# Decode attention with a gated GeGLU: w_gate loaded ahead of wq, the first keys in two loads

## The chip, the cores and the metric

The kernel runs on one core of a Trainium2 chip. Its time is the device time of one execution in microseconds (us); a profiled execution shows where the time goes. Engines: TensorE (PE; PEld is its weight load), VectorE (DVE), ScalarE (ACT), GpSimd (POOL) and SyncE (SP), which here issues nearly all transfers.

## The reference

```
x [4, 1, 512]; k_cache, v_cache [4, 32, 4096, 128]; wq [512, 4096]; wo [4096, 512]
w_gate, w_up [512, 1792]; w_down [1792, 512]; gate_w [512]; all float32

q = (x @ wq) as [4, 32, 1, 128]
p = softmax(q . k_cache / sqrt(128))
a = (p . v_cache) as [4, 1, 4096] @ wo
b = (gelu_tanh(x @ w_gate) * (x @ w_up)) @ w_down
g = sigmoid(sum(x * gate_w))
out = g * a + (1 - g) * b
```

## The kernel before

The caches are 537 of the 565 MB that are read. They are cut into NT = 32 pieces of keys and 32 of values, 8.39 MB each: piece i holds four heads of one batch row, as 128 partitions x 16384 elements (128 rows of 128). The texts call the loads k0, k1, ... and v0, v1, ...

All big data live in one tile `big` with 45056 elements per partition. A key piece lies at 0 (even i) or 12288 (odd i); so two neighbours share the quarter from 12288 to 16384. The values lie at VA = 28672. A step's work on its keys is split for this: `products(i, True)` and `sums(i, True)` multiply the shared quarter by the query and add up (VectorE), then SP issues the load of k(i+1), which overwrites it, and `products(i, False)` and `sums(i, False)` do the other three quarters. `soft_max(i)` then makes the weights, on VectorE and ACT. `pv(i - 1)` multiplies the values by them on TensorE, and v(i) is issued when it is done, into the same place.

Before the first step: `q_project` (x @ wq, 64 matmuls on TensorE), four operations on VectorE (L347 to L352, and L368), `q_spread` (TensorE) and a copy to the tile `qb` (ACT, L374), after which the first product (L384) can start. The feed-forward's `ffn_up(0)` and `ffn_up(1)` (x @ w_gate, x @ w_up, 32 matmuls each, L518), `gates` and `ffn_gelu` (L530 to L537) stand inside step 0, between its two sums.

wq lies in the place of the values. w_gate and w_up go into the same place, so their loads wait for `q_project`. v0 goes there too and waits for `ffn_gelu`. The results of `ffn_up` go to `fu`, two pieces of `big` behind w_up.

A planner (`Plan`) writes the program: each engine's instructions stand in the order in which they are called, and every step gets the semaphore waits that its reads and writes of places in tiles need. SP issues its loads in the written order too, so a load that waits holds up those behind it. All loads are put on one queue, shared by 16 DMA engines.

Of the kernel before, what the change touches and what calls it, by code (L numbers as in the profile page):

```python
# [8 lines left out]
AF = mybir.ActivationFunctionType  # L9
OP = mybir.AluOpType  # L10
# [122 lines left out]
def tile_gated_mix(tc: tile.TileContext, x, kc, vc, wq, wo, w_gate, w_up, w_down, gate_w, out):  # L133
    nc = tc.nc
    P = 128
    B, H, S, D = kc.shape
    DM = x.shape[2]
    F = w_gate.shape[1]
    KC = DM // P
# [6 lines left out]
    TW = R * D  # L146
    RO = R // 4
    RJ = 4
    BP = 2
    FG = F // 4  # L150
    FC = F // P
    HW = 16
    E = HW * D // P
# [15 lines left out]
    def sb(pool, name, shape):  # L169
        sizes[name] = math.prod(shape[1:])  # L170
        return pool(name, [P] + list(shape[1:]), F32).ap()[:shape[0]]
# [6 lines left out]
    KB_, VA = TW - RO * D, 2 * TW - RO * D  # L178
# [8 lines left out]
    half = sb(consts, "half", [P, 1])  # L187
# [14 lines left out]
    O = [sb(consts, f"o{n}", [P, RJ, D]) for n in range(B // BP)]  # L202
# [6 lines left out]
    q = sb(ps, "q", [P, B, D])  # L209
# [3 lines left out]
    sm = sb(ps, "sm", [P, D + 1])  # L213
    sg = sb(ps, "sg", [P, KC * B])

    Q0, F0, F1, W0, D0 = VA, VA, VA + KC * F, VA, VA + TW // 2
    W1, ES = TW, TW + TW // 2
    GS = VA - 6 * DM
    XS, U0, QD, FU, FT, OXA = VA - 2 * DM, VA - 4 * DM, VA - DM, VA + 2 * KC * F, ES + 2 * E * 32, ES + 2 * E * 32 + DM

    def place(a, n):
        return big[:, a:a + n]

    def z(a, n):
        return ("big", a, a + n)

    def t(*names):
        return [(n, 0, sizes[n]) for n in names]
# [3 lines left out]
    x_sb, gw = place(XS, DM)[:B], place(GS, DM)[:B]  # L232
    u = place(U0, 2 * DM).rearrange("p (s n) -> p s n", s=2)
    qd = place(QD, D)
    fu = place(FU, 2 * DM).rearrange("p (s n) -> p s n", s=2)
    OX32 = place(OXA, E * GW * HT * D // E)[:32].rearrange("q (e g h k) -> q e g h k", e=E, g=GW, h=HT)
    OX = OX32[:B * HT]
    oV = place(FT, E * 32).rearrange("p (e m) -> p e m", e=E)
# [5 lines left out]
    V, A, T, G = nc.vector, nc.scalar, nc.tensor, nc.gpsimd  # L244

    def dve(emit, reads, writes):
        return add("dve", emit, reads, writes)

    def act(emit, reads, writes):
        return add("act", emit, reads, writes)  # L250

    def pe(emit, reads, writes):
        return add("pe", emit, reads, writes)
# [4 lines left out]
    def load(dst, src, writes, lane):  # L258
        return add("sp", lambda: nc.sync.dma_start(dst, src), (), writes, lane=lane, unit=16)

    def load_kv(kind, i):
        src = (vc, kc)[kind == "k"]
        a = KB_ * (i % 2) if kind == "k" else VA if i < NT - 1 else 0
        s = src[i % B, HT * (i // B):HT * (i // B) + HT].rearrange("h (p r) d -> (h p) (r d)", p=PH)
        load(place(a, TW), s, [z(a, TW)], "vl" if kind == "v" and i == NT - 1 else kind)

    def KA(i):
# [5 lines left out]
    def load_f(s):  # L273
        load(place((F0, F1)[s], KC * F), (w_gate, w_up)[s].rearrange("(p c) n -> p (c n)", c=KC),
             [z((F0, F1)[s], KC * F)], f"f{s}")
# [4 lines left out]
    def load_w(w):  # L280
# [4 lines left out]
        if w:  # L285
            for h in range(2):
                for e in range(WO_END[w][-1], E):
                    n0, m = e * DM + COLS[2 * h][0], COLS[2 * h + 1][1] - COLS[2 * h][0]
                    load(place(W1 + n0, m), src[:, n0:n0 + m], [z(W1 + n0, m)], f"e{h}{e % 2}")

    load(place(Q0, KC * H * D), wq.rearrange("(p c) n -> p (c n)", c=KC), [z(Q0, KC * H * D)], "q")
    add("act", lambda: nc.scalar.dma_start(x_sb, x.rearrange("b s d -> (b s) d")), (), [z(XS, DM)], lane="x0", unit=16)
    add("act", lambda: nc.scalar.dma_start(gw, gate_w.rearrange("(s n) -> s n", s=1).to_broadcast([B, DM])), (),
# [61 lines left out]
    def gates():  # L355
        pe(lambda: T.matmul(sm[:, :B], ones[:B], gd, start=True, stop=True), t("ones", "gd"), [("sm", 0, B)])
        act(lambda: A.activation(g4, sm[:, :B], AF.Exp, scale=-1.0), [("sm", 0, B)], t("g4"))
        dve(lambda: V.tensor_scalar(g4, g4, 1.0, None, op0=OP.add), t("g4"), t("g4"))
        dve(lambda: V.reciprocal(g4, g4), t("g4"), t("g4"))
        dve(lambda: V.tensor_tensor(g16.rearrange("p (j b) -> p j b", b=B), m16.rearrange("p (j b) -> p j b", b=B),  # L360
                                    g4[:, None, :].to_broadcast([P, 4, B]), op=OP.mult), t("m16", "g4"), t("g16"))
        dve(lambda: V.tensor_reduce(g1, g16, axis=AX.X, op=OP.add), t("g16"), t("g1"))
        dve(lambda: V.tensor_scalar(half, g1, -0.5, 0.5, op0=OP.mult, op1=OP.add), t("g1"), t("half"))
        dve(lambda: V.tensor_tensor(gmask, g4[:, :, None].to_broadcast([P, B, HT]),
                                    pmask[:, None, :].to_broadcast([P, B, HT]), op=OP.mult), t("g4", "pmask"), t("gmask"))

    def q_pick(g):
        dve(lambda: V.tensor_scalar(HC, hmask[:, bass.ds(row(g - 1) * HT + HT, HT), None].to_broadcast([P, HT, PH]), 1.0,  # L368
                                    None, op0=OP.mult), t("hmask"), t("hc"))

    def q_spread():
        pe(lambda: T.matmul(q.rearrange("p b d -> p (b d)"), HC.rearrange("p h k -> p (h k)"),  # L372
                            QM.rearrange("p b d -> p (b d)"), start=True, stop=True), t("hc", "QM"), t("q"))
        act(lambda: A.activation(QB, q, AF.Copy), t("q"), t("qb"))  # L374
# [4 lines left out]
    def products(i, shared):  # L379
        b = i % B  # L380
        r0, r1 = rows(i, shared)
        k = place(KA(i), TW).rearrange("p (r d) -> p r d", d=D)[:, r0:r1]
        m = [z(KA(i) + r0 * D, (r1 - r0) * D)]
        dve(lambda: V.tensor_tensor(k, k, QB[:, b:b + 1, :].to_broadcast([P, r1 - r0, D]), op=OP.mult),  # L384
            m + t("qb"), m)

    def sums(i, shared):
        r0, r1 = rows(i, shared)
        k = place(KA(i), TW).rearrange("p (r d) -> p r d", d=D)[:, r0:r1]
        dve(lambda: V.tensor_reduce(SC[i % 2][:, r0:r1], k, axis=AX.X, op=OP.add),  # L390
            [z(KA(i) + r0 * D, (r1 - r0) * D)], [(f"sc{i % 2}", r0, r1)])
# [30 lines left out]
    def gather_a(i):  # L422
        n = i // BP % 2
        act(lambda: A.activation(O[n], PO[n], AF.Copy), t(f"po{n}"), t(f"o{n}"))  # L424
# [89 lines left out]
    def ffn_up(s):  # L514
        def emit():
            for c in range(KC):
                for j in range(4):
                    last = T.matmul(q.rearrange("p b d -> p (b d)")[32 * j:32 * j + 32, :FG], xTf[:, c, :32],  # L518
                                    place((F0, F1)[s] + c * F + j * FG, FG), start=c == 0, stop=c == KC - 1)
            return last  # L520

        pe(emit, t("xT") + [z((F0, F1)[s], KC * F)], t("q"))
        act(lambda: A.activation(fu[:, s, :FG], q.rearrange("p b d -> p (b d)")[:, :FG], AF.Copy),
            t("q"), [z(FU + s * DM, FG)])

    def ffn_gelu():
        x1, r1 = fu[:, 0, :FG], [z(FU, FG)]
        (t1, z1), (t2, z2), (t3, z3), (th, z4), (y, z5), (v, z6) = (
            (place(F1 + a * DM, FG), [z(F1 + a * DM, FG)]) for a in range(6))
        dve(lambda: V.tensor_tensor(t1, x1, x1, op=OP.mult), r1, z1)  # L530
        dve(lambda: V.tensor_scalar(t2, t1, 0.044715, 1.0, op0=OP.mult, op1=OP.add), z1, z2)
        dve(lambda: V.tensor_tensor(t3, t2, x1, op=OP.mult), z2 + r1, z3)
        act(lambda: A.activation(th, t3, AF.Tanh, scale=c_gelu), z3, z4)
        dve(lambda: V.scalar_tensor_tensor(y, th, 1.0, x1, op0=OP.add, op1=OP.mult), z4 + r1, z5)  # L534
        dve(lambda: V.scalar_tensor_tensor(v, y, half, fu[:, 1, :FG], op0=OP.mult, op1=OP.mult),  # L535
            z5 + t("half") + [z(FU + DM, FG)], z6)
        dve(lambda: V.transpose(hT, v.rearrange("p (k i) -> p i k", i=FC)), z6, t("hT"))  # L537

    def ffn_down(f0, f1):
# [1 line left out]
            a = D0 + f * DM  # L541
            project_wide(hT[:, f, :], place(a, DM), [("hT", f * 32, f * 32 + 32), z(a, DM)])

    load_f(0)
    load_f(1)
    q_pick(0)
    q_spread()
    for i in range(NT):
        g, b = divmod(i, B)
        plan.turn = (i - 1) // B if 0 < i < NT - B + 1 else None  # L550
        if b == 1 and g + 1 < NG:
            q_pick(g + 1)
        products(i, True)
        sums(i, True)
        if i < NT - 1:
            load_kv("k", i + 1)
        else:
            load_kv("v", i)
        products(i, False)
        if i == 0:  # L560
            gates()
            ffn_up(0)
            ffn_up(1)
            ffn_gelu()
            load_kv("v", 0)
        sums(i, False)
        if i > 0:
            pv(i - 1)
            if i < NT - 1:
                load_kv("v", i)  # L570
            if i % BP == 0:
                gather_a(i - 1)
            if b == 0:
                gather(g - 1)
            if b == 3 and g + 1 < NG:
                q_spread()
        soft_max(i)
        if i > 0 and b == 0:
            weigh(g - 1)
# [25 lines left out]
    for h in range(2):  # L605
        for e in range(WO_END[1][-1], E):
            s, w, reads = attended(1, e)
# [52 lines left out]
```

## Time and profile before

| | |
|---|---|
| time, median of 3 runs | 1308.96 us (1308.88 to 1309.77) |
| the profiled execution | 1308.95 us, its span 1307.5 us |
| busy: VectorE | 1158.2 us |
| busy: TensorE, its weight loads | 353.2, 100.2 us |
| busy: ACT | 87.3 us |
| transfers | 564.83 MB, 432 GB/s over the span |

The span is the part of an execution that the trace covers, 1.45 us shorter than the time. Busy times of different engines overlap.

### The profile page before, as it was taken

The page shows a single profiled execution, that of the slowest core. Times are in us where ns is not written, and L with a number is a line of the kernel's source. Part 1 is how long each engine was busy: PE and PEld are TensorE (multiplying, and loading weights), DVE is VectorE, ACT ScalarE, POOL GpSimd, SP SyncE. Part 2 cuts the span into 40 slices and gives each one's busy share as a digit, 9 for nine tenths or more (in the row PEclk, how much of TensorE's full clock was granted, in tenths as well). Part 3 has the DMA queues.
Part 4 walks back from the last instruction along what each step waited for, and adds up shares of the span by engine and source line. Part 5 has one row for each costly group of instructions (what it writes and reads, how often), then busy time and mean ns, then how long its engine had stood idle before and what let it go on. Part 6 is the DMA issues. An engine that isn't in the chain of part 4 may idle for free.

```text
span 1307.5 us, 6158 instructions
## 1 busy us (share of the span) xinstructions
PE 353.2 (27%) x2512; PEld 100.2 (8%) x2512; DVE 1158.2 (89%) x303; ACT 87.3 (7%) x291; POOL 0.7 (0%) x6
## 2 busy tenths in 40 slices
PE   2303233212232211322321222321133232123227
PEld 0100001000010000100000000100001000000003
DVE  2799999999899998989989898998989899898992
ACT  0000000000000000000000000000000000000001
POOL 0000000000000000000000000000000000000000
PEclk9656666556666656666655666665666665666668
DMA  9999999999999999999999999999999999999998
GB/s 418 424 439 439 430 441 428 439 427 441 425 441 425 441 427 439 435 433 439 431 439 429 439 427 441 425 441 425 441 433 433 439 431 439 431 439 428 439 428 370
DMA packets 10986, 564.83 MB, mean 432 GB/s; under 512 B 1232, under 2 KB 1752, under 8 KB 1888
## 3 DMA queue, kind: packets, MB, share of 16 engines
q1 hardware_dynamic: 10960, 564.67, 99.8%
q8 instruction: 7, 0.11, 0.0%
q14 instruction: 3, 0.02, 0.0%
q10 hardware_dynamic: 16, 0.02, 0.0%
HBM read 564.67 MB, written 0.01 MB: 432 GB/s over the span
## 4 chain that ended last, share of the span: by engine, by line
DMA 72%; DVE 26%; PE 1%; issue 1%; ACT 0%; SPq 0%; DVEq 0%
DMA big<-in_A_k_cache 66%; DVE sc L390 13%; DVE big L384 12%; DMA big<-in_B_w_up 2%; DMA big<-in_A_wo 2%; DMA big<-in_A_wq 2%; PE po L330 1%; PE q L518 0%; PE acc L505 0%; PE wide L497 0%; PE po L505 0%; DVE hT L537 0%; DVE big L535 0%; DVE big L530 0%; DVE big L534 0%
## 5 line engine op out<-in xcount | busy, mean ns | idle before, releaser
L384 DVE TENSOR_TENSOR big<-big,qb 128x4096 f32<-128x4096 f32 x64 | 556.0, 8687 | 89.5 <-DMA big<-in_A_k_cache 89.5
L390 DVE TENSOR_REDUCE sc<-big 128x32 f32<-128x4096 f32 x64 | 555.9, 8686 | 2.3
L416 PE MATMUL po<-big,PM 128*32 128x512 f32 x2048 | 295.9, 743 | 899.9 <-DMA big<-in_A_v_cache 899.9
L416 PEld LDWEIGHTS po<-big,PM 128*32 128x32 f32 x2048 | 72.7, 133 | 1116.7 <-DMA big<-in_A_v_cache 823.9
L402 ACT ACTIVATE PM<-sc,nb 32x128 f32<-32x128 f32 x128 | 67.2, 525 | 476.4 <-DVE nb L397 430.7
L424 ACT ACTIVATE o<-po 128x512 f32<-128x512 f32 x16 | 9.6, 597 | 446.2 <-PE po L416 446.2
L402 ACT ACTIVATION_READ_ACCUMULATOR PM<-sc,nb 32x1 f32 x128 | 26.1, 204 | 0.0
L374 ACT ACTIVATE qb<-q 128x512 f32<-128x512 f32 x8 | 4.8, 597 | 245.7 <-PE q L372 245.7
L347 DVE TENSOR_TENSOR big<-po,amask 128x512 f32<-128x512 f32 x2 | 1.3, 686 | 18.0 <-PE po L330 18.0
L433 PE MATMUL sm<-o,sel 128*16 128x128 f32 x128 | 15.4, 273 | 5.8 <-ACT o L424 5.8
L518 PE MATMUL q<-big,xT 128*32 128x448 f32 x64 | 9.5, 751 | 18.0 <-DMA big<-in_B_w_gate 13.0
L330 PE MATMUL po<-big,xT 128*32 128x512 f32 x64 | 8.7, 702 | 18.9 <-DMA big<-in_A_wq 18.9
L433 PEld LDWEIGHTS sm<-o,sel 128*16 128x16 f32 x128 | 11.7, 97 | 14.4 <-ACT o L424 13.1
L615 DVE COPY res<-acc 4x144 f32<-4x144 f32 x1 | 0.3, 296 | 12.7 <-PE acc L505 12.7
L372 PE MATMUL q<-QM,hc 128*128 128x512 f32 x16 | 9.3, 666 | 4.2 <-DVE hc L368 4.2
L395 DVE TENSOR_REDUCE m<-sc 128x1 f32<-128x128 f32 x32 | 9.2, 286 | 1.1
L440 DVE RECIPROCAL ri<-sm 16x1 f32<-16x1 f32 x8 | 1.2, 156 | 8.7 <-PE sm L435 8.7
L396 DVE STREAM_TRANSPOSE mt<-m 128x32 f32<-128x32 f32 x32 | 6.8, 212 | 1.1
L397 DVE TENSOR_REDUCE nb<-mt 128x1 f32<-128x32 f32 x32 | 5.9, 186 | 1.1
L497 PE MATMUL wide<-big 128*32 128x512 f32 x46 | 5.6, 596 | 1.9 <-DMA big<-in_A_wo 1.9
L320 DVE TENSOR_TENSOR big<-big 4x512 f32<-4x512 f32 x1 | 0.7, 679 | 4.8 <-DMA big<-in_gate_w 4.8
L518 PEld LDWEIGHTS q<-big,xT 128*32 128x32 f32 x64 | 2.9, 146 | 23.8 <-issue 23.8
(74 smaller groups left out, 59.8 us busy)
## 6 DMA issues: line engine op xcount, KB each, us to landing
big<-in_A_wo SPq DMA_DIRECT2D x1, 4096.0 KB, 28.3
big<-in_B_w_gate SPq DMA_DIRECT2D x1, 3584.0 KB, 18.9
big<-in_B_w_up SPq DMA_DIRECT2D x1, 3584.0 KB, 28.1
big<-in_B_w_down SPq DMA_DIRECT2D x1, 3584.0 KB, 19.0
big<-in_A_wo SPq DMA_DIRECT2D x1, 1792.0 KB, 26.4
big<-in_A_wo SPq DMA_DIRECT2D x1, 1280.0 KB, 29.1
big<-in_A_k_cache SPq DMA_DIRECT2D x32, 29.7
big<-in_A_v_cache SPq DMA_DIRECT2D x32, 29.3
```

Of the source, the lines that this page charges most:

```text
L330: last = T.matmul(PO[s][32 * j:32 * j + 32].rearrange("p j d -> p (j d)"), xTf[:, c, :32], w[:, n0:n0 + HB * D], start=c == 0, stop=c == K ...
L372: pe(lambda: T.matmul(q.rearrange("p b d -> p (b d)"), HC.rearrange("p h k -> p (h k)"), QM.rearrange("p b d -> p (b d)"), start=True, sto ...
L384: dve(lambda: V.tensor_tensor(k, k, QB[:, b:b + 1, :].to_broadcast([P, r1 - r0, D]), op=OP.mult), m + t("qb"), m)
L390: dve(lambda: V.tensor_reduce(SC[i % 2][:, r0:r1], k, axis=AX.X, op=OP.add), [z(KA(i) + r0 * D, (r1 - r0) * D)], [(f"sc{i % 2}", r0, r1)])
L395: dve(lambda: V.tensor_reduce(M1[n], SC[n], axis=AX.X, op=OP.max), t(f"sc{n}"), t(f"m1{n}"))
L396: dve(lambda: V.transpose(MT, M1[n].to_broadcast([P, PH])), t(f"m1{n}"), t("mt"))
L397: dve(lambda: V.tensor_reduce(NB[n], MT, axis=AX.X, op=OP.max, negate=True), t("mt"), t(f"nb{n}"))
L402: last = A.activation(PM[:, PZ:].rearrange("p (c m) -> p c m", m=32)[s, :, h:RJ * HT:HT], SC[n][s, :].rearrange("p (c j) -> p c j", j=RJ), ...
L416: last = T.matmul(PO[n][32 * c:32 * c + 32].rearrange("p j d -> p (j d)"), PM[:, m0:m0 + 32], place(VAT(i) + j * N, N), start=b == 0 and j ...
L424: act(lambda: A.activation(O[n], PO[n], AF.Copy), t(f"po{n}"), t(f"o{n}"))
L433: T.matmul(sm[:B * HT, :D], selv[:, j, m0:m0 + B * HT], O[n][:, j, :], start=(n, j) == (0, 0), stop=(n, j) == (N - 1, RJ - 1))
L518: last = T.matmul(q.rearrange("p b d -> p (b d)")[32 * j:32 * j + 32, :FG], xTf[:, c, :32], place((F0, F1)[s] + c * F + j * FG, FG), start ...
```

## The change

w_gate (`load_f(0)`) is issued first of all, ahead of wq; it goes to the place F0 = TW = 16384, inside the place of k1, which is free until then. Behind wq, k0 comes in two loads: the shared quarter (elements 12288 to 16384 of each row), which the first product reads, and the other three quarters. w_up alone waits for `q_project` and goes to VA. `ffn_up(0)` is written right behind the first `q_spread`. The results of `ffn_up` go to the tiles `o0` and `o1`, which `gather_a` fills in later steps.

```diff
-    Q0, F0, F1, W0, D0 = VA, VA, VA + KC * F, VA, VA + TW // 2
+    Q0, F0, F1, W0, D0 = VA, TW, VA, VA, VA + TW // 2
...
-    fu = place(FU, 2 * DM).rearrange("p (s n) -> p s n", s=2)
+    fu = [O[s].rearrange("p j d -> p (j d)")[:, :FG] for s in range(2)]
...
+        if kind == "k" and i == 0:
+            for c0, c1 in ((TW - RO * D, TW), (0, TW - RO * D)):
+                load(place(a + c0, c1 - c0), s[:, c0:c1], [z(a + c0, c1 - c0)], "k" if c0 else "k0")
+            return
         load(place(a, TW), s, [z(a, TW)], "vl" if kind == "v" and i == NT - 1 else kind)
...
+    load_f(0)
     load(place(Q0, KC * H * D), wq.rearrange("(p c) n -> p (c n)", c=KC), [z(Q0, KC * H * D)], "q")
...
-        act(lambda: A.activation(fu[:, s, :FG], q.rearrange("p b d -> p (b d)")[:, :FG], AF.Copy),
-            t("q"), [z(FU + s * DM, FG)])
+        act(lambda: A.activation(fu[s], q.rearrange("p b d -> p (b d)")[:, :FG], AF.Copy),
+            t("q"), [(f"o{s}", 0, FG)])
...
-    load_f(0)
     load_f(1)
     q_pick(0)
     q_spread()
+    ffn_up(0)
...
         if i == 0:
             gates()
-            ffn_up(0)
             ffn_up(1)
             ffn_gelu()
             load_kv("v", 0)
```

The first loads on SP, before (in_A_k_cache is k0, then k1 and k2; in_A_v_cache is v0; lane_pe and lane_dve are the semaphores that TensorE and VectorE raise):

```order
L259 DMA big<-in_A_wq 128x16384
L259 DMA big<-in_A_k_cache 128x16384
L627 UNCONDITIONAL_BRANCH
L259 DMA big<-in_B_w_gate 128x7168 [waits barrier_Pool_Activation_PE_DVE_SP_release,lane_pe]
L259 DMA big<-in_B_w_up 128x7168
L259 DMA big<-in_A_k_cache 128x16384 [waits lane_dve]
L259 DMA big<-in_A_v_cache 128x16384 [waits lane_dve]
L259 DMA big<-in_A_k_cache 128x16384 [waits lane_dve]
```

and with the change:

```order
L259 DMA big<-in_B_w_gate 128x7168
L259 DMA big<-in_A_wq 128x16384
L259 DMA big<-in_A_k_cache 128x4096
L259 DMA big<-in_A_k_cache 128x12288
L631 UNCONDITIONAL_BRANCH
L259 DMA big<-in_B_w_up 128x7168 [waits barrier_Pool_Activation_PE_DVE_SP_release,lane_pe]
L259 DMA big<-in_A_k_cache 128x16384 [waits lane_pe,lane_dve]
L259 DMA big<-in_A_v_cache 128x16384 [waits lane_dve]
L259 DMA big<-in_A_k_cache 128x16384 [waits lane_dve]
```

Four loads instead of two go out without a wait, one instead of two waits for `q_project`, and k1 waits for TensorE too.

TensorE up to the first loop, before (L330 is `q_project`, L372 `q_spread`, L356 the matmul of `gates`, L518 `ffn_up`):

```order
L330 MATMUL po<-big,xT 32x512 [waits lane_q,lane_dve]
L330 MATMUL po<-big,xT 32x512 x31
L372 MATMUL q<-QM,hc 128x512 [waits lane_dve]
L356 MATMUL sm<-gd,ones 128x4
L518 MATMUL q<-big,xT 32x448 [waits lane_f0,lane_act]
L518 MATMUL q<-big,xT 32x448 x15
L518 MATMUL q<-big,xT 32x448 [waits lane_f1,lane_act]
L518 MATMUL q<-big,xT 32x448 x15
```

and with the change, where all line numbers here are 5 higher:

```order
L335 MATMUL po<-big,xT 32x512 [waits lane_q,lane_dve]
L335 MATMUL po<-big,xT 32x512 x31
L377 MATMUL q<-QM,hc 128x512 [waits lane_dve]
L523 MATMUL q<-big,xT 32x448 [waits lane_f0,lane_act]
L523 MATMUL q<-big,xT 32x448 x15
L361 MATMUL sm<-gd,ones 128x4
L523 MATMUL q<-big,xT 32x448 [waits lane_f1,lane_act]
L523 MATMUL q<-big,xT 32x448 x15
```

`ffn_up(0)` now stands ahead of the matmul of `gates`.

## Rows read from the trace of the kernel before

**Rows 1.** The page: busy us (share of the span) and instructions; transfers.

```profile
span 1307.5 us, 6158 instructions
PE 353.2 (27%) x2512; PEld 100.2 (8%) x2512; DVE 1158.2 (89%) x303; ACT 87.3 (7%) x291; POOL 0.7 (0%) x6
...
DMA packets 10986, 564.83 MB, mean 432 GB/s; under 512 B 1232, under 2 KB 1752, under 8 KB 1888
```

**Rows 2.** Table by stretch; columns as in its first row.

```profile
core 0: us, PE busy (x) PEld busy (x) DVE busy (x) ACT busy (x) POOL busy (x), PEclk, DMA share, GB/s
...
79.30:98.70 19.40, 0.03 (x4) 0.03 (x4) 19.22 (x8) 2.12 (x8) 0.00 (x0) 0.50 1.00 433
98.70:118.00 19.30, 9.95 (x64) 2.31 (x64) 19.27 (x2) 0.00 (x0) 0.00 (x0) 0.68 1.00 435
...
234.10:1200.00 965.90, 248.03 (x1720) 67.68 (x1720) 887.29 (x193) 63.43 (x218) 0.00 (x0) 0.62 1.00 434
```

**Rows 3.** Waits of VectorE: waited for, us in total, times, longest.

```profile
DVE big L384 <- DMA big<-in_A_k_cache: 89.5, 30, 6.5
```

**Rows 4.** Timeline of the value matmuls (`pv`): start, us, what [idle before].

```profile
98.67 9.98 PE L416 MATMUL po<-big,PM 128*32 128x512 f32 x64 [33.61 <-DMA big<-in_A_v_cache]
137.27 9.46 PE L416 MATMUL po<-big,PM 128*32 128x512 f32 x64 [28.62 <-DMA big<-in_A_v_cache]
...
214.67 10.01 PE L416 MATMUL po<-big,PM 128*32 128x512 f32 x64 [28.70 <-DMA big<-in_A_v_cache]
...
330.58 8.38 PE L416 MATMUL po<-big,PM 128*32 128x512 f32 x64 [29.69 <-DMA big<-in_A_v_cache]
```

**Rows 5.** Timeline of SP's issues up to k2.

```profile
0.74 0.40 SPq L259 DMA_DIRECT2D big<-in_A_wq  x1
...
31.91 0.43 SPq L259 DMA_DIRECT2D big<-in_B_w_up  x1
50.99 0.33 SPq L259 DMA_DIRECT2D big<-in_A_k_cache  x1
69.82 0.33 SPq L259 DMA_DIRECT2D big<-in_A_v_cache  x1
92.50 0.33 SPq L259 DMA_DIRECT2D big<-in_A_k_cache  x1
```

**Rows 6.** Timeline of all engines from 60 to 66 us.

```profile
60.16 4.90 PE L518 MATMUL q<-big,xT 128*32 128x448 f32 x32 [4.99 <-DMA big<-in_B_w_up]
...
65.12 0.63 DVE L530 TENSOR_TENSOR big<-big 128x448 f32<-128x448 f32 x1 [0.31 <-PE q L518]
```

**Rows 7.** Timeline of all engines from 22 to 55 us.

```profile
22.82 8.66 PE L330 MATMUL po<-big,xT 128*32 128x512 f32 x64 [18.93 <-DMA big<-in_A_wq]
...
31.54 1.29 DVE L347 TENSOR_TENSOR big<-po,amask 128x512 f32<-128x512 f32 x2 [17.97 <-PE po L330]
...
37.16 0.60 ACT L374 ACTIVATE qb<-q 128x512 f32<-128x512 f32 x1 [33.41 <-PE q L372]
...
42.08 4.43 DVE L384 TENSOR_TENSOR big<-big,qb 128x4096 f32<-128x4096 f32 x1 [6.48 <-DMA big<-in_A_k_cache]
...
50.61 4.56 PE L518 MATMUL q<-big,xT 128*32 128x448 f32 x32 [12.97 <-DMA big<-in_B_w_gate]
```

**Rows 8.** Table by stretch inside the first value matmuls, columns as in rows 2.

```profile
98.60:105.00 6.40, 6.33 (x32) 1.50 (x36) 6.40 (x1) 0.00 (x0) 0.00 (x0) 0.53 1.09 471
105.00:108.70 3.70, 3.65 (x36) 0.84 (x28) 3.67 (x2) 0.00 (x0) 0.00 (x0) 1.00 0.74 319
```

**Rows 9.** The chain that ended last: start, us, what (transfers from their issue).

```profile
0.74 21.94 DMA big<-in_A_wq
...
127.93 28.80 DMA big<-in_A_k_cache
...
165.67 29.66 DMA big<-in_A_k_cache
195.33 0.02 issue
195.35 4.44 DVE big L384
```

**Rows 10.** Timeline of SP at the end.

```profile
1305.72 0.81 SPq L616 DMA_DIRECT2D out<-res  x2
```

More of the change, by code (lines that the diff above doesn't have):

```diff
@@ L214, in tile_gated_mix @@
     sg = sb(ps, "sg", [P, KC * B])
-    Q0, F0, F1, W0, D0 = VA, VA, VA + KC * F, VA, VA + TW // 2
+    Q0, F0, F1, W0, D0 = VA, TW, VA, VA, VA + TW // 2
     W1, ES = TW, TW + TW // 2
     GS = VA - 6 * DM
-    XS, U0, QD, FU, FT, OXA = VA - 2 * DM, VA - 4 * DM, VA - DM, VA + 2 * KC * F, ES + 2 * E * 32, ES + 2 * E * 32 + DM
+    XS, U0, QD, FT, OXA = VA - 2 * DM, VA - 4 * DM, VA - DM, ES + 2 * E * 32, ES + 2 * E * 32 + DM
     def place(a, n):
@@ L522, in ffn_up @@
         pe(emit, t("xT") + [z((F0, F1)[s], KC * F)], t("q"))
-        act(lambda: A.activation(fu[:, s, :FG], q.rearrange("p b d -> p (b d)")[:, :FG], AF.Copy),
-            t("q"), [z(FU + s * DM, FG)])
+        act(lambda: A.activation(fu[s], q.rearrange("p b d -> p (b d)")[:, :FG], AF.Copy),
+            t("q"), [(f"o{s}", 0, FG)])
     def ffn_gelu():
-        x1, r1 = fu[:, 0, :FG], [z(FU, FG)]
+        x1, r1 = fu[0], [("o0", 0, FG)]
         (t1, z1), (t2, z2), (t3, z3), (th, z4), (y, z5), (v, z6) = (
@@ L534, in ffn_gelu @@
         dve(lambda: V.scalar_tensor_tensor(y, th, 1.0, x1, op0=OP.add, op1=OP.mult), z4 + r1, z5)
-        dve(lambda: V.scalar_tensor_tensor(v, y, half, fu[:, 1, :FG], op0=OP.mult, op1=OP.mult),
-            z5 + t("half") + [z(FU + DM, FG)], z6)
+        dve(lambda: V.scalar_tensor_tensor(v, y, half, fu[1], op0=OP.mult, op1=OP.mult),
+            z5 + t("half") + [("o1", 0, FG)], z6)
         dve(lambda: V.transpose(hT, v.rearrange("p (k i) -> p i k", i=FC)), z6, t("hT"))
```

## The prediction

> **What bounds the kernel now.** I read the page's summary first. VectorE is busy 1158.2 us of a span of 1307.5, TensorE 353.2, and the transfers move 564.83 MB at a mean of 432 GB/s [rows 1]. Two candidates remain, VectorE and the transfers. The table by stretch decides: whatever the engines do, the 16 DMA engines are at a share of 1.00 and at 433 to 435 GB/s in the stretches of one load each, and also over the 965.9 us in the middle; VectorE is idle for 78.6 us of those [rows 2]. VectorE waits 30 times for keys, 89.5 us in all [rows 3]. One key load and one value load (2 x 8.39 MB) take 38.6 us, as the starts of the value matmuls at 98.67 and 137.27 show [rows 4]; that is 19.3 us a load. So the end is set by one queue of bytes that never runs dry. No order of loads makes it shorter; it gets longer where a load is issued after the load ahead of it has ended. What must be read from the trace is therefore, for each early load, how long before the end of its predecessor SP issues it.
>
> SP's rows give that [rows 5]. k1 (the second keys) is issued at 50.99, while w_up ends where TensorE starts on it, at 60.16 [rows 6]: 9 us ahead. v0 (the first values) is issued at 69.82 behind a k1 that ends 19.3 us after w_up, at 79.4: 9.6 ahead. k2 is issued at 92.50, and v0 is all there at 98.67 [rows 4]: 6.2 ahead. This last is the tightest.
>
> The end of a load as a matmul sees it is that of the slowest of the 16 engines. From the landing of k0 at 42.08 [rows 7] to the end of v0 the queue holds w_gate, w_up, k1 and v0, 24.1 MB, at 435 GB/s 55.4 us: on the mean the engines are done at 97.5, the last 1.2 us later. For an engine to be fed, k2 must be there by 97.5 rather than by 98.67.
>
> **The change part by part.** *w_gate in front.* The same 3.67 MB, so nothing over the whole. wq lands later by what w_gate takes: 50.61 - 42.08 = 8.5 us, the gap between the landing of k0 and TensorE's start on w_gate [rows 7]. q_project, at 22.82 now, starts at 31.3.
>
> *The query chain.* From q_project's start VectorE and TensorE make the query, and ACT has it spread over all partitions at 37.16 + 0.60 = 37.76 [rows 7], 14.9 us after the start. With the change that is 46.3. Now this chain is hidden: VectorE waits 6.48 us for the keys until 42.08. After, the first quarter of k0 lands at 31.3 + 19.3/4 = 36.1 and all of it at 50.6, so the quarter waits for the query and not the reverse. VectorE's first product moves from 42.08 to 46.3, 4.2 us later. The splitting of k0 is needed for no more than this: with k0 whole it would start at 50.6.
>
> q_project's length is the uncertain part. It took 8.7 us with a cold start. The value matmuls, 64 of the same width, took 8.38 to 10.01 us [rows 4], by how long they ran at a granted clock near half: 32 took 6.33 us at 0.53, 36 took 3.65 us at 1.00 [rows 8], that is the 1.2 and the 2.4 GHz level. I take the middle, 9.2; then the first product starts at 46.8 (46.0 to 47.6).
>
> *ffn_up(0) moved ahead on TensorE.* Its w_gate landed long before (at about 12: the wq load's 21.94 from 0.74 [rows 9], less the 10.9 by which w_gate is the smaller). It runs behind the query's spread, 4.6 us long [rows 7], at about 47 to 52, beside VectorE's first product and sum. k1's place now holds w_gate, so SP waits for this too; the first sum ends later (below), so it costs nothing. The gate's small matmul behind it is asked for 20 us later.
>
> *VectorE's work up to k2.* From the first product to k2's issue there are 92.50 - 42.08 = 50.4 us of VectorE without a wait but 0.31 us for ffn_up(1) [rows 5 to 7]. With the change w_up is issued when q_project is done (about 40.5), sits behind k0, and lands at 50.6 + 8.5 = 59.1 to 60.2; its matmuls end by 65.1, ahead of VectorE's gates, now at about 68. The 0.3 goes away: 50.1 us. Writing the results of ffn_up to the o tiles is the same copy as to the big tile; the o tiles are first needed two turns later.
>
> *The three leads after the change.* k1: issued at 46.8 + 8.9 = 55.7, w_up ends at 59.1 at the earliest: 3.4 us ahead, still more than a start costs (below). v0: 46.8 + 27.7 - 0.3 = 74.2, k1 ends at 78.4 on the mean: 4.2 ahead. k2: 46.8 + 50.1 = 96.9, against a mean end of v0 of 97.5, as before, since the same bytes stand ahead of it: 0.6 ahead.
>
> *What a start costs.* An issue is not data. The first load of the kernel took 21.94 us from its issue [rows 9] against 19.3 in a stream: 2.6 us at most from issue to flow. The two output transfers go out in a 0.81 us stretch from 1305.72 [rows 10] and the span ends at 1307.5, with their landing: 1.8 us for issue and landing together. A bound from below is the issue itself, 0.33 us [rows 5]. I take 1.5 us, near the output's. k2 flows at 98.4, and the engines are dry for 98.4 - 97.5 = 0.9 us. Low end: 96.1 + 0.33, no gap. High end: 97.7 + 2.6 - 97.5 = 2.8 us.
>
> *The extra load.* 128 more rows. w_gate's 128 rows of 28 KB took 8.5 us where 7/16 of 19.3 is 8.4 [rows 4, 7]; so under 0.1 us, and I take 0.1. If each load paid for its own start, the price would be the 2.6 us of the first one; the landing of w_gate only 8.5 us behind k0 speaks against it while the queue is fed. [...]
>
> *After k2.* VectorE is late against the keys for a turn or two more. k3: 127.93 - 92.50 = 35.4 us later [rows 5, 9], at 132.3; the v1 ahead of it ends at 137.27 + 0.9 [rows 4]: ahead by 4 on the mean. A turn of VectorE is 35.4 to 36 us and one of the queue 38.6, so it has caught up by the fourth keys (195.35 in the row [rows 9]).
>
> **Sum.** 0.9 + 0.1 = +1.0 us on the profiled execution's 1308.95, which is also the median (1308.96): 1310.0 us. A difference of 0.2%, 2.6 us, is about what a measurement can tell here; this is within it.
>
> **Rivals.**
> - *Full cover* (0.33): k2 at 96.1 to 96.9 comes before the engines are done, or the engines that are 1 us behind set the end anyway. 1309.0. For it: the last engine ends at 98.67; against it: the start costs something, and the mean engine is free at 97.5.
> - *The lateness stays whole* (0.04): VectorE's 4.2 - 0.3 = 3.9 us go straight to the end, 1312.9, slower. It decides if VectorE has no slack in later turns; against it stand the 89.5 us that it waits for keys [rows 3].
> - *A slow q_project* (0.05): if TensorE stays at the 1.2 GHz level, 64 matmuls take 64 x 6.33/32 = 12.7 us; the first product starts at 50.3, k1 flows at 60.7 and k2 at 101.9, 4.4 us dry: 1313.5, slower by 0.3%. The point is q_project over 10.9 us (k2's issue over 98.6). Against it: the longest of the value matmuls shown took 10.01.
> - *A cheaper opening* (0.05): the 2.6 us of the first load shrink with the smaller w_gate in front. Half of it gone and no gap gives 1307.7, half of what 0.2% needs; nothing in the rows says which part of the 2.6 goes with the size of the rows.
> - *A price per load* (0.02): the load more costs the 2.6 us of a first start even in a fed queue, beside the gap: 1308.95 + 0.9 + 2.6 = 1312.5, slower. Against it: w_gate's 8.5 us behind k0. [...]
>
> **How the numbers follow.** The forecast (a gap of 0.3 to 2.6 us) has 0.51. Slower by over 0.2% are the lateness, the slow q_project and the price per load: 0.11. Faster by as much is only an opening that gives back all of its 2.6 us: 0.02 of its 0.05. The rest is within 0.2%: 0.87. The range of 8 in 10 runs from full cover, less 0.5 for the opening, 1308.5, to the high end of the gap with the extra load and some of the spread of the runs before (up to 1309.77), 1312.5.
>
> **What would show it.** q_project starting at 31.3; the first product's wait ending on the query, not on keys, at 46 to 47.6; SP issuing k1 near 55.5, v0 near 74, k2 near 97; the matmuls on v0 starting at 98.7 as before, and those on v1 at 138 to 139 instead of 137.27. From there all is shifted by the same amount, the tail too. Wrong would be: v1 at 137.3 (full cover), k1 or v0 found dry, a shift that still grows after the fourth keys, or a q_project outside 8.4 to 10.0.

## The result and the profile after

The changed kernel takes 1311.47 us (median of 18 runs, 1310.08 to 1312.48), the kernel before 1308.95 (18 runs, 1308.82 to 1309.77): a ratio of 1.0018, 95% interval 1.0011 to 1.0025. It is 2.5 us slower, just inside the 2.6 us named as the bound, and its runs lie 2.4 us apart instead of 0.95. The profiled execution took 1310.12, one of the shortest.

The page after, answering [rows 1]: the same bytes at the same mean rate, VectorE as busy as before.

```profile
span 1308.8 us, 6160 instructions
PE 350.3 (27%) x2512; PEld 99.6 (8%) x2512; DVE 1158.1 (88%) x303; ACT 87.3 (7%) x291; POOL 0.7 (0%) x6
...
DMA packets 11130, 564.83 MB, mean 432 GB/s; under 512 B 1248, under 2 KB 1768, under 8 KB 1904
```

The timeline of TensorE, ACT, VectorE and SP after, answering [rows 5, 7], shows the query's chain from q_project to the issues of k1, v0 and k2:

```profile
31.33 8.88 PE L335 MATMUL po<-big,xT 128*32 128x512 f32 x64 [26.38 <-DMA big<-in_A_wq]
...
40.28 1.29 DVE L352 TENSOR_TENSOR big<-po,amask 128x512 f32<-128x512 f32 x2 [29.70 <-PE po L335]
...
44.39 1.24 PE L377 MATMUL q<-QM,hc 128*128 128x512 f32 x2 [4.18 <-DVE hc L373]
45.67 0.60 ACT L379 ACTIVATE qb<-q 128x512 f32<-128x512 f32 x1 [40.85 <-PE q L377]
46.30 4.42 DVE L389 TENSOR_TENSOR big<-big,qb 128x4096 f32<-128x4096 f32 x1 [1.96 <-ACT qb L379]
...
55.21 0.33 SPq L259 DMA_DIRECT2D big<-in_A_k_cache  x1
...
73.64 0.33 SPq L259 DMA_DIRECT2D big<-in_A_v_cache  x1
...
96.31 0.33 SPq L259 DMA_DIRECT2D big<-in_A_k_cache  x1
```

The first product (L389) waited for the keys before; now its wait ends on the query, at 46.30 instead of 42.08. k2 is issued at 96.31 instead of 92.50, 50.0 us behind it.

What that does to the queue stands in a table of 1 us stretches (columns as in [rows 2]; the last two are the DMA share and GB/s; a row of a load is counted whole where it starts, so that a share can be over 1). After:

```profile
96.00:97.00 1.00, 0.00 (x0) 0.00 (x0) 1.00 (x2) 0.00 (x0) 0.00 (x0) 0.50 0.00 0
97.00:98.00 1.00, 0.00 (x0) 0.00 (x0) 1.00 (x1) 0.00 (x0) 0.00 (x0) 0.50 2.09 721
98.00:99.00 1.00, 0.00 (x0) 0.00 (x0) 1.00 (x1) 0.00 (x0) 0.00 (x0) 0.50 0.79 328
```

and before:

```profile
96.00:97.00 1.00, 0.00 (x0) 0.00 (x0) 1.00 (x1) 0.00 (x0) 0.00 (x0) 0.50 1.67 721
97.00:98.00 1.00, 0.00 (x0) 0.00 (x0) 1.00 (x1) 0.00 (x0) 0.00 (x0) 0.50 0.46 197
98.00:99.00 1.00, 0.33 (x4) 0.20 (x8) 1.00 (x1) 0.00 (x0) 0.00 (x0) 0.50 0.30 131
```

Before, 11 rows of 64 KB start between 96 and 97 (721 GB/s in 1 us); after, none starts there, and 11 start between 97 and 98. They also take longer: a share of 2.09 for the bytes that took 1.67, a quarter more. So k2's lateness has two costs, a dry queue and slow first rows.

The value matmuls after, answering [rows 4] (timeline of TensorE): 98.67 became 99.29, 137.27 became 137.93, and the last but one, on v30, which stood at 1258.00, is 1.5 us later. The 0.6 us on v0 can't come from k2, which stands behind v0 in the queue; why v0 landed late on its slowest engine in this execution is not shown.

```profile
99.29 9.04 PE L421 MATMUL po<-big,PM 128*32 128x512 f32 x64 [35.35 <-DMA big<-in_A_v_cache]
137.93 8.49 PE L421 MATMUL po<-big,PM 128*32 128x512 f32 x64 [29.60 <-DMA big<-in_A_v_cache]
...
177.43 9.22 PE L421 MATMUL po<-big,PM 128*32 128x512 f32 x64 [31.01 <-DMA big<-in_A_v_cache]
...
1259.50 9.20 PE L421 MATMUL po<-big,PM 128*32 128x512 f32 x64 [28.92 <-DMA big<-in_A_v_cache]
```

From the third (176.08 before) on the shift is 1.35 to 1.6 us, and the last of all, on v31, starts at 1278.80 instead of 1277.62; the time of the execution rose by as much, 1.2 us. The middle runs at the same 434 GB/s [rows 2].

```profile
98.70:118.00 19.30, 9.04 (x64) 2.19 (x64) 19.27 (x2) 0.00 (x0) 0.00 (x0) 0.77 1.00 435
234.10:1200.00 965.90, 247.38 (x1720) 67.60 (x1720) 887.29 (x192) 63.37 (x219) 0.00 (x0) 0.63 1.00 434
```

### The profile page after: what moved, and what is told of

Same layout as the page of the kernel before. It is cut to its first block, busy times and chain, and to the rows that moved or that the text cites. A ratio compares the mean times of both kernels' runs of the same rounds, so it can differ in the third digit from the quotient of the medians.

```text
span 1308.8 us, 6160 instructions
## 1 busy us (share of the span) xinstructions
PE 350.3 (27%) x2512; PEld 99.6 (8%) x2512; DVE 1158.1 (88%) x303; ACT 87.3 (7%) x291; POOL 0.7 (0%) x6
## 4 chain that ended last, share of the span: by engine, by line
DMA 68%; DVE 30%; PE 1%; issue 1%; ACT 0%; SPq 0%; DVEq 0%
DMA big<-in_A_k_cache 64%; DVE big L389 15%; DVE sc L395 14%; DMA big<-in_A_wq 2%; DMA big<-in_A_wo 2%; PE po L335 1%; PE acc L510 0%; PE wide L502 0%; DVE big L355 0%; DVE big L352 0%; PE q L377 0%; PE po L510 0%; DVE hT L542 0%; DVE m L400 0%; DVE big L540 0%
## 5 line engine op out<-in xcount | busy, mean ns | idle before, releaser
L389 DVE TENSOR_TENSOR big<-big,qb 128x4096 f32<-128x4096 f32 x64 | 555.9, 8687 | 82.7 <-DMA big<-in_A_k_cache 80.8
L502 PE MATMUL wide<-big,hT 128*32 128x512 f32 x28 | 3.9, 597 | 0.0
```

Source lines behind the costliest of these rows:

```text
L502: pe(lambda: T.matmul(wide[32 * c:32 * c + 32, :], s, w, start=n < 4, stop=n >= NW - 4), reads, t("wide"))
```

## The experiments

The theory: the change moves VectorE's start behind the query, so k2 is issued too late to find the queue filled, and each microsecond of lateness past some point is a microsecond at the end. The rivals: the opening with w_gate costs something; a load more costs something; all of VectorE's lateness counts. Times are medians, with their range and the ratio's interval to the kernel before, whose median beside them was 1309.06 for e1, e2, e4_warm and e5, and 1308.98 for e3a, e3b, e4b and e6.

**wq first again** (e1_wq_first), all else as changed:

```diff
-    load_f(0)
     load(place(Q0, KC * H * D), wq.rearrange("(p c) n -> p (c n)", c=KC), [z(Q0, KC * H * D)], "q")
+    load_f(0)
```

> The changed kernel with one thing undone: wq is issued first again and w_gate behind it (both without a wait); the split of k0, the early ffn_up(0) and the place of its results stay. Theory (the query is late, so VectorE issues k2 after the engines have emptied the queue): q_project starts at 22.8 again, the query is there at 37.8, k2 is issued near 91.5 (ffn_up(1) then holds VectorE for some 3 us), at least 5 us ahead of the end of v0: 1309.0, with the small spread of before. Rival, a price per load or per part of k0: the loads are as many as in the changed kernel, so 1310 to 1311.5 stays. Rival, a dearer opening with w_gate: 1309.0 too.

1309.03 (1308.83 to 1309.24), ratio 0.9991 to 1.0009. The first product starts at 39.80 (q_project and the spread were slow in this execution), and VectorE then waits 3.0 us for the rest of k0, not for ffn_up(1) as I had written. k2, 1.4 us behind its forecast, is in time:

```profile
92.91 0.33 SPq L259 DMA_DIRECT2D big<-in_A_k_cache  x1
```

All the loss is tied to w_gate standing ahead of wq; the split, the moved ffn_up(0) and the o tiles cost nothing that shows. That leaves the theory and the opening.

**k0 whole** (e2_k0_whole), all else as changed:

```diff
-        if kind == "k" and i == 0:
-            for c0, c1 in ((TW - RO * D, TW), (0, TW - RO * D)):
-                load(place(a + c0, c1 - c0), s[:, c0:c1], [z(a + c0, c1 - c0)], "k" if c0 else "k0")
-            return
```

> The changed kernel with k0 in one load. Theory: the first product then waits for all of k0, at 50.7 instead of 46.3; k2 is issued at 100.8, flows at about 102.4, and the engines, empty at 97.35 on the mean, are dry for 5.0 us, and their first rows together are slow by another 0.55 as at the opening: 1314.6, with the small spread of before, as the query is no longer what VectorE waits for. k1 (issued at 59.6) finds the queue dry too. Rival, a price per load: one load less, so 1309 to 1310. Rival, all of VectorE's lateness goes to the end: 8.6 - 0.3 us, 1317.3.

1315.07 (1314.79 to 1315.17), ratio 1.0032 to 1.0059. The first product waits for keys again, and k2 is issued at 100.70, 0.1 us from the forecast. One load less and 3.6 us slower than the changed kernel: without the split, w_gate in front would have cost 6.0 us. A fixed start of the opening can't do this.

```profile
50.69 4.43 DVE L385 TENSOR_TENSOR big<-big,qb 128x4096 f32<-128x4096 f32 x1 [5.31 <-DMA big<-in_A_k_cache]
```

k1 is late too, as was expected: TensorE starts on w_up, which stands ahead of k1, before k1 is issued.

```profile
59.20 3.22 PE L519 MATMUL q<-big,xT 128*32 128x448 f32 x16 [4.55 <-DMA big<-in_B_w_up]
59.60 0.33 SPq L259 DMA_DIRECT2D big<-in_A_k_cache  x1
```

**The split alone** (e5_split_only), on the kernel before:

```diff
+        if kind == "k" and i == 0:
+            for c0, c1 in ((TW - RO * D, TW), (0, TW - RO * D)):
+                load(place(a + c0, c1 - c0), s[:, c0:c1], [z(a + c0, c1 - c0)], "k" if c0 else "k0")
+            return
```

> The kernel before with k0 in two loads, the shared quarter first, and nothing else changed: the price of a load more. Theory: the first product starts at 37.8, ffn_up(1) still ends at 65, so k2 is issued at 92.5 as before: 1309.0 (128 rows more, under 0.1 us). Rival, a price per load: 1310.5 to 1311.5.

1309.06 (1308.79 to 1309.61), ratio 0.9991 to 1.0009; k2 at 91.00, a little earlier than before. A load more in a fed queue has no price that shows. The Trainium skill ("DMA: Bandwidth & Descriptors", "Anatomy of one DMA — SWDGE (gpsimd) path") fits about 2.0 us plus the bytes to a DMA on GpSimd's path; these loads are issued by SP, so no run here tests that fit.

**VectorE made late in the kernel before** (e3a_delay8, e3b_delay15), by 8 and 15 writes of zeros in step 0:

```diff
             load_kv("v", i)
+        if i == 0:
+            for n in range(8):
+                dve(lambda: V.memset(res, 0.0), (), t("res"))
         products(i, False)
```

> The kernel before, loads and all, with 8 writes of zeros to the idle tile res on VectorE between the first sum and the second product of step 0: about 4.2 us more on VectorE, and nothing else. Theory: k2 is issued at 96.4, as in the changed kernel's profile, and the time rises as there, by about 1.1 us (0.55 dry, 0.5 for slow first rows), to 1310.1, with a smaller spread than the changed kernel's, because VectorE here starts from the landing of k0 and not from q_project. Rivals, the price per load, the opening with w_gate: 1309.0, no load differs.

> The same with 15 writes, about 7.8 us more. Theory: k2 is issued at 100.0, flows at 101.6 on the mean where the engines are empty at 97.35: 4.2 dry and 0.5 for slow first rows, 1313.7. Rival, VectorE's lateness counts in full from the start: 1316.5, and 1313.0 with 8 writes; rivals, price per load or opening: 1309.0.

1311.62 (1311.30 to 1312.35; ratio 1.0012 to 1.0030) and 1316.11 (1315.79 to 1316.66; ratio 1.0041 to 1.0069), 1.5 and 2.4 us above what was expected. Each write cost 0.66 us with its wait, not 0.52, so k2 was issued at 97.58 and 101.81, not at 96.4 and 100.0. The loads are those of before, in its order: lateness of VectorE alone makes the loss. The opening and the price per load are out as the cause. That lateness counts in full is out too: 5.1 us (97.58 - 92.50) cost 2.6, the rest was slack.

The table by stretch (columns as above) of the first of the two shows the restart cleanly, since all 16 engines are empty:

```profile
97.00:98.00 1.00, 0.00 (x0) 0.00 (x0) 1.00 (x2) 0.00 (x0) 0.00 (x0) 0.50 0.00 0
98.00:99.00 1.00, 0.32 (x4) 0.20 (x8) 1.00 (x1) 0.00 (x0) 0.00 (x0) 0.50 3.16 1049
```

and of the second, a stretch in which 16 rows start in a fed queue:

```profile
95.00:96.00 1.00, 0.00 (x0) 0.00 (x0) 1.00 (x1) 0.00 (x0) 0.00 (x0) 0.50 2.42 1049
```

The 16 rows are the same 1049 GB/s x 1 us; they take 3.16 us on the mean after a dry queue, 2.42 in a fed one: 0.74 us more. A narrower stretch of the first run shows how long a start takes: k2 is issued at 97.58, and all 16 rows start 0.9 to 1.4 us later.

```profile
97.58:98.50 0.92, 0.00 (x0) 0.00 (x0) 0.92 (x1) 0.00 (x0) 0.00 (x0) 0.50 0.00 0
98.50:99.00 0.50, 0.32 (x4) 0.20 (x8) 0.50 (x1) 0.00 (x0) 0.00 (x0) 0.50 6.33 2097
```

In the second run v0 is late as well. It is issued at 79.13, none of its rows starts before 80, and then all 16 start together, as slow as those of k2 in the first run:

```profile
79.13 0.33 SPq L259 DMA_DIRECT2D big<-in_A_v_cache  x1
80.00:81.00 1.00, 0.00 (x0) 0.00 (x0) 1.00 (x1) 0.00 (x0) 0.00 (x0) 0.50 3.21 1049
```

**Half of q_project** (e6_half_q): the changed kernel with half of x @ wq left out.

```diff
-        for c in range(KC):
+        for c in (0, KC - 1):
             w = place(Q0 + c * H * D, H * D)
```

> The changed kernel with q_project cut to two of its four blocks of wq (half of x @ wq is left out; all loads stay). Theory: q_project takes 4.5 to 6.4 us, the query is ready some 3.5 us earlier, k2 is issued at 92 to 94, before the engines are empty: 1309.0, and the spread is that of before, 0.9 us or less. Rivals, the opening, the price per load, the moved ffn_up(0): 1311.5 with a spread of 2.4.

1309.11 (1308.90 to 1309.75), ratio 0.9992 to 1.0010; the runs lie 0.85 us apart. q_project took 6.22 us, and k2 is issued at 94.55 (92 to 94 expected), 1.8 us earlier than in the changed kernel; with w_gate in front and all loads as changed, the loss and the scatter of the runs are gone:

```profile
94.55 0.33 SPq L259 DMA_DIRECT2D big<-in_A_k_cache  x1
```

**TensorE kept busy ahead of q_project** (e4_warm, and e4b_warm_longer with 8 more of the matmuls on w_gate):

```diff
+    def warm():
+        for n in range(5):
+            for c in range(KC):
+                for j in range(4):
+                    last = T.matmul(q.rearrange("p b d -> p (b d)")[32 * j:32 * j + 32, :FG], xTf[:, c, :32],
+                                    place(F0 + c * F + j * FG, FG), start=c == 0, stop=c == KC - 1)
+        return last
+
+    pe(warm, t("xT") + [z(F0, KC * F)], t("q"))
     pe(q_project, t("xT") + [z(Q0, KC * H * D)], t("po0", "po1"))
```

> The changed kernel with 80 more matmuls on w_gate ahead of q_project (their result is not used), which keep TensorE busy from about 12 to 29 us, so that q_project starts at the 2.4 GHz level. Theory: q_project takes 6.9 us instead of 8.9, the first product starts at 44.4, k2 is issued at 94.4 and flows at 95.5 to 96.5, before the engines are empty at 97.0: 1309.1, and the spread of the changed kernel (2.4 us) shrinks to that of before (0.9). Rivals, the opening or the price per load: 1311.5 as the changed kernel, with its spread.

> The changed kernel with 88 unused matmuls on w_gate ahead of q_project where the run before had 80, so that TensorE is busy until q_project starts (there it stood idle for 2.9 us and fell to the 1.2 GHz level inside q_project). Theory: q_project takes 6.9 to 7.2 us; the first product starts at 44.3, or at 45.6 if wq again lands 1.2 us late on one engine; k2 is issued at 94.4 to 95.7: 1309.1 to 1309.9. Rivals, the opening or the price per load: 1311.5 or above.

Both missed what I had expected: 1312.60 (1311.13 to 1313.28; ratio 1.0014 to 1.0036) and 1311.56 (1310.01 to 1312.23; ratio 1.0009 to 1.0027). In the first, TensorE stood idle for 2.9 us ahead of q_project and the granted clock then fell to the 1.2 GHz level inside it (table by stretch; 0.53 in the second row):

```profile
32.60:34.10 1.50, 1.50 (x12) 0.41 (x16) 0.00 (x0) 0.00 (x0) 0.00 (x0) 0.84 0.99 426
34.10:37.20 3.10, 3.10 (x20) 0.85 (x16) 0.00 (x0) 0.00 (x0) 0.00 (x0) 0.53 1.24 534
37.20:41.40 4.20, 4.16 (x40) 1.04 (x32) 0.00 (x0) 0.00 (x0) 0.00 (x0) 1.00 1.01 437
```

In the second, q_project is as short as was expected, but wq itself is there only at 32.54, 1.2 us later than in the changed kernel, and the query's spread ran at a granted clock of 0.53 (timeline of TensorE):

```profile
32.54 7.08 PE L335 MATMUL po<-big,xT 128*32 128x512 f32 x64 [1.53 <-DMA big<-in_A_wq]
43.79 1.99 PE L386 MATMUL q<-QM,hc 128*128 128x512 f32 x2 [4.18 <-DVE hc L382]
```

So the chain came out no shorter (k2 at 98.29 and 96.45), and the attempt to set the clock didn't work. Why wq landed late in both is not shown. The table of queues for the stretch from 12 to 33 us has one 16 KB transfer of instructions in both of these runs and none in the changed kernel; that would hold up one of the 16 engines, but I didn't test it.

**The changed kernel three times more** (r1_after_again to r3_after_again), without an edit, for the scatter of its runs:

> The changed kernel once more, for where its spread of 2.4 us is from. So far each profiled run's time stood on one line against the moment at which SP issues k2: 1310.12 at 96.31, 1311.42 at 97.58, 1312.89 at 98.29, 1314.79 at 100.70, 1315.79 at 101.81. Theory: this run falls on the same line (about 1309.8 + 1.03 for each us of k2's issue after 96.0), and k2's issue differs from 96.31 by what q_project and the query's spread differ from 8.88 and 1.24 us, which the TensorE clock sets. Rival, the spread is the transfers' own: the time differs, k2's issue doesn't.

> As for the run before it: on the line, with q_project between 8.4 and 10.0 us and k2's issue between 95.8 and 98.0.

> As for the run before it: on the line, with q_project between 8.4 and 10.0 us and k2's issue between 95.8 and 98.0.

1309.98, 1311.90 and 1310.68, with k2 issued at 96.27, 97.95 and 96.29. The first two fall on the line of the expectation, the third 0.6 us above it. The timeline of the second, the slowest, shows both of TensorE's pieces long, q_project and the query's spread:

```profile
31.32 9.70 PE L335 MATMUL po<-big,xT 128*32 128x512 f32 x64 [26.40 <-DMA big<-in_A_wq]
45.20 2.08 PE L377 MATMUL q<-QM,hc 128*128 128x512 f32 x2 [4.18 <-DVE hc L373]
```

All profiled executions together, by k2's issue:

| run | k2 issued | time of this execution |
|---|---|---|
| e5_split_only | 91.00 | 1308.79 |
| before | 92.50 | 1308.95 |
| e1_wq_first | 92.91 | 1308.84 |
| e6_half_q | 94.55 | 1309.04 |
| r1_after_again | 96.27 | 1309.98 |
| r3_after_again | 96.29 | 1310.68 |
| after | 96.31 | 1310.12 |
| e4b_warm_longer | 96.45 | 1311.56 |
| e3a_delay8 | 97.58 | 1311.42 |
| r2_after_again | 97.95 | 1311.90 |
| e4_warm | 98.29 | 1312.89 |
| e2_k0_whole | 100.70 | 1314.79 |
| e3b_delay15 | 101.81 | 1315.79 |

Flat up to 94.55, then a line: from the changed kernel's own profile to the last row 5.67 us for 5.50 us of issue. A straight line through the nine rows from 96.27 on has a slope of 0.97 and meets 1308.95 at 94.7; no row lies between 94.55 and 96.27, so 94.7 is where the line ends and not a measured edge. In e2 and e3b the queue ran dry twice, but in every row the same bytes stand ahead of k2, so its issue counts both gaps. The nine rows lie within 0.9 us of the line, e4b farthest. What that residue is made of stays open; the late landing of wq on some engine is the candidate in e4b.

## Why the prediction was right, and where its sizes were off

*The mechanism* held. q_project started at 31.33 (31.3 forecast), the first product's wait ended on the query, k1 and v0 were issued at 55.21 and 73.64 (55.5 and 74 forecast), ahead of their predecessors' ends, k2 was the load that came late, and the shift grew by only 0.2 us after the third value load. Two signs were missed: the matmuls on v0 started 0.6 us later than the 98.7 forecast, and those on v1 at 137.93, just short of the 138 to 139. The experiments show that VectorE's lateness is the cost, and no other cost of the change shows in them: the loss goes when the query comes earlier (e1, e6), grows when VectorE is later (e2), and appears in the kernel before when VectorE alone is delayed (e3a, e3b). The early ffn_up(0) and the o tiles, put at nothing, cost nothing that shows (e1, e6), nor did the extra load, put at 0.1 (e5).

*The size* was 1.0 us where 2.5 were measured, by two terms. That the forecast came as near as it did is in part luck.

The term "what a start costs" held only the dry time. At k2's forecast issue, 96.9, the line gives 1311.1, 1.1 us above my sum. Of these, 0.74 is what the first rows after a dry queue take longer (3.16 against 2.42). I had the same thing before me in the first load, issued at 0.74, and took all of its 2.6 us for latency; the table by stretch of the kernel before shows that its first 16 rows start from 1 us after the issue on and take 3.04 us on the mean:

```profile
1.70:2.70 1.00, 0.00 (x0) 0.00 (x0) 0.13 (x1) 0.23 (x1) 0.20 (x1) 1.00 3.04 1053
```

The dry time itself, 0.9 us, rests on two values that were both too late by about 0.4 us and so cancelled. A start takes 0.9 to 1.4 us (e3a) and not 1.5. And the engines are empty earlier than the mean of 97.5, which I had counted from 42.08, itself the landing on the slowest engine: in the kernel before, 11 of k2's first 16 rows start between 96 and 97, 3 in the next microsecond and 2 in the one after, at about 97 on the mean. Some 0.4 us of the 1.1 stay unexplained.

The query's chain was the other. I let q_project vary between 8.4 and 10.0 us, and so it does (8.40 to 9.70 in four profiles of the changed kernel), but held the spread at its one row of 1.47. It takes 1.24 to 2.08 in these profiles, and longer where less of the clock was granted (table by stretch: the shortest, in the changed kernel's profile, and the longest, in r2):

```profile
44.39:45.63 1.24, 1.24 (x2) 0.30 (x2) 0.00 (x0) 0.00 (x0) 0.00 (x0) 0.86 0.55 238
45.20:47.28 2.08, 2.08 (x2) 0.50 (x2) 0.00 (x0) 0.00 (x0) 0.00 (x0) 0.50 0.87 378
```

Over q_project the same column reads 1.00 in all four, so what sets its length is not shown. The median of 1311.47 stands on the line at an issue of 97.3, 0.4 us later than my 96.9. These two pieces can also make most of the scatter of the runs. As an estimate, their longest values together would put k2 at about 98.3 (10.0, nearly reached by the 9.99 in e1, + 2.08 against 8.88 + 1.24, on 96.31), 1312.5 by the line, and the slowest of the 18 runs took 1312.48. In e2, where the first product waits for keys and not for TensorE, 5 runs lie only 0.38 us apart. But r1, r3 and the changed kernel's profile lie 0.7 us apart with k2 issued within 0.04 us, so a part of the scatter is not the chain's.

*The rivals.* Full cover, at 0.33, was too likely: in no profile of the changed kernel was k2 early enough, and 94.7, where the line ends, would have needed a chain 1.6 us shorter. The whole lateness was refuted by e3a, the price per load by e5. A cheaper opening can't be told apart from nothing: w_gate first in e6 gives the time of before. A q_project over 10.0 us was not seen.

## What to carry to other kernels

When one queue of transfers is the bound, look for the load with the smallest lead over the end of its predecessor, and cost every edit by what it does to that lead; work that the queue hides is free only up to there. Here a delay of VectorE was paid only past an issue time about 4 us ahead of the last landing of the load in front (94.7 by the line, against 98.67): engines run empty one by one, a start takes about 1 us, and the first rows after it are slow. A wait that moves from a transfer to a chain over TensorE also takes on the scatter of that chain: the changed kernel has runs 2.4 us apart instead of 0.95. None of these versions beats the kernel before, which keeps its queue full.

## What the runs showed of the hardware

In e3a and e3b, 16 rows of 64 KB that start together after an empty queue took 3.16 and 3.21 us on the mean, against 2.42 for 16 in a fed queue; in e3a they started 0.9 to 1.4 us after the issue. Two 128-wide matmuls of 512 float32 columns, the query's spread, took 1.24 us at a granted clock of 0.86 and 2.08 at 0.50 in two executions of one kernel. Keeping TensorE busy until 2.9 us before q_project did not keep it at the 2.4 GHz level: the granted clock was 0.84 over the first 1.5 us of q_project and 0.53 over the next 3.1.
